# An FFT convolution and MLP kernel: the inverse transforms of two blocks folded once more on VectorE

## The chip, the cores and the metric

The kernel runs on one core of a Trainium2 chip. The core has a matrix engine (TensorE, PE in the profile, with PEld for its weight loads), VectorE (DVE), ScalarE (ACT), GpSimd (POOL) and SyncE (SP), which here only issues transfers. Each engine works through its own queue in order; waits between queues go over semaphores. The metric is the time of one execution on the device in microseconds, lower is better.

## The reference

The input is a sequence of 2048 positions with 512 channels in bf16. Two layers are applied, and in both the same weights and the same `A_k`, `A_v` are used. A layer is a long convolution gated by the normalized input, and then an MLP:

```python
k_shift = sum over t of k_pad[:, t:t + S, :] * shift_k[:, ks - 1 - t]   # 4 taps
kv = k_shift * v
y = irfft(rfft(kv_pad) * rfft(ssm_k_pad))[:S] + kv * ssm_D
x = x + layernorm(x) * y
x = x + (gelu(layernorm(layernorm(x)) @ w1 + b1) @ w2 + b2)    # 512 -> 1376 -> 512
```

The convolution result `y` depends on `k`, `v`, `ssm_k`, `ssm_D` alone, not on `x`, so it is the same in both layers and is computed once.

## The kernel before

**Tiling.** The sequence is cut into 4 blocks of 512 positions. A block lies in SBUF as 128 partitions by 4 positions (position 4p + i on partition p, i = 0 to 3) by 512 channels. The convolution is done by blocks in the frequency domain with a transform of 1024 points of which each block fills half. `forward` (L577 on) turns a block into 256 complex frequencies with matmuls against a table (`R_F`); they lie in two groups of 128 frequencies, numbered c = 0 and 1, each with a real and an imaginary half of 512 channels (ri = 0, 1). Before the change group 0 holds the frequencies 2n + 1/2 and group 1 those at 2n + 3/2. `wrap` joins the spectra of neighbouring filter blocks, `products` multiplies and sums spectra, `inverse` goes back to time with matmuls against a second table (`R_T`) and copies the result to `R_YT`.

**Stages and tags.** In the recorded program each step has a tag: S*b* the shift of block b, K*b* its forward transform, H*m* the spectrum of filter block m, W*m* its wrap, P*b*c0 and P*b*c1 the products of each frequency group, P*b*e the step that combines the products and splits them into two parities o = 0, 1 (time index even or odd), Y*b* the inverse. M*bL*a0 and a1 are the norms and transposes of the MLP of block b in layer L (first and second half of the block), M*bL*b the two matrix products.

**Products.** Block b sums b + 1 products; the first goes straight to the accumulator `R_ACC`, each further one goes to a scratch slot and is added by a DMA that GpSimd issues (L620, `accumulate`). The combining step P*b*e at the end of `products` is four VectorE operations of 2048 elements per partition for blocks 1 to 3 (two groups at once) by the helper `tt` (L557).

**Inverse.** For each half h of the time indices `inverse` issues matmuls of 128x512 over o, c and ri (L575, helper `freq`): 8 per half, 16 per block. The two halves are two PSUM tiles, and ScalarE copies each (L563).

**The MLP.** L779 normalizes on ScalarE, L807 transposes, L824 is the first product (44 matmuls of 512 columns per block, or 88 of 256 where the block is done in halves), L829 the Gelu on ScalarE, L843 the second product (44), L848 (layer 0) and L851 (layer 1) the residual on VectorE. Statistics are L750 and L752 on VectorE; the variance goes to GpSimd for a power of -1/2 (L738; its input is made by L755, L757 or L773) and comes back to VectorE, which makes the shift of the normalization (L739).

**What sets the order.** All operations are recorded first, with what they read and write. `ORDER` is a list of their numbers written out in the file: each engine's queue is the list's operations of that engine in the list's sequence. `BANKS` gives each PSUM tile its bank, and `SIDE` lists the copies that go to VectorE where ScalarE is the default (`copy` with two engines). `replay` runs through the queues with a table of costs to set the waits, and `keep_busy` (its matmul is L913) puts idle matmuls of 128x512 into TensorE's queue where, by those costs, it would stand still for over 700 ns: `k = int(gap * share / cost)`, share 0.8, cost 217.

## Time and profile before

| | |
|---|---|
| median of 3 runs | 245.62 us (245.22 to 245.80) |
| the profiled execution | 244.91 us |
| its span, first to last instruction | 243.1 us |
| TensorE busy, matmuls | 232.9 us, 1551 |
| VectorE busy, instructions | 185.1 us, 357 |
| ScalarE busy, instructions | 181.6 us, 279 |
| mean granted TensorE clock | 0.999 |

A row of the timeline gives the start in us, the time to the end of the last of the merged instructions, the engine, the line, the operation, output and input, the count, and in brackets the idle time just ahead and what ended it. Instructions of one engine overlap a little in the records, so the time from one start to the next is what one costs in a full queue. A row of a stretch (from:to) gives its length, the busy time of PE, PEld, DVE, ACT and POOL with their instruction counts, the granted clock, the share of time in which DMA engines were busy, and GB/s. Busy shares are averages over stages that differ.

### The profile page before, as it was taken

Reading aid. Unit: us, or ns where it says so; the run is one execution under the profiler, and the core shown is the slowest. Engines: PE = TensorE matmul, PEld = TensorE weight load, DVE = VectorE, ACT = ScalarE, POOL = GpSimd, SP = SyncE. Lnnn points to the kernel's source line nnn. Section 1 sums busy time; section 2 is a strip of 40 time slices with the busy share of each in tenths; the row PEclk is TensorE's granted clock in tenths of the full one; section 3 lists DMA queues with packets and bytes.
Section 4 is the critical chain, followed back from the end, with each engine's and each line's share of the span. In section 5 each row is a group of like instructions: output and inputs, shape, how many; then the busy total and the mean of one; then the engine's idle time right before and its main releaser. Section 6 shows DMA issues by size and latency. Waiting matters only on the chain.

```text
span 243.1 us, 3962 instructions
## 1 busy us (share of the span) xinstructions
PE 232.9 (96%) x1551; PEld 131.9 (54%) x1574; DVE 185.1 (76%) x357; ACT 181.6 (75%) x279; POOL 68.0 (28%) x73
## 2 busy tenths in 40 slices
PE   8999996989999999999999999999999999999994
PEld 3756632647655684445444544544468654448841
DVE  1379999999999999999999999783977242574004
ACT  2358998999899589979799285579968657955730
POOL 0000134432572356753146315241310201120000
PEclk9999999999999999999999999999999999999999
DMA  6999916668794099990089989920002000002002
GB/s 189 392 377 220 391 52 238 105 242 162 142 158 62 0 173 173 175 174 3 0 162 185 172 215 226 207 47 3 1 0 89 0 0 3 0 0 86 3 0 86
DMA packets 14406, 29.85 MB, mean 123 GB/s; under 512 B 3026, under 2 KB 8500, under 8 KB 14260
## 3 DMA queue, kind: packets, MB, share of 16 engines
q0 software_dynamic: 5232, 15.21, 32.9%
q1 hardware_dynamic: 9156, 14.40, 17.2%
q8 instruction: 12, 0.20, 0.3%
q14 instruction: 6, 0.05, 0.1%
HBM read 12.30 MB, written 2.10 MB: 59 GB/s over the span
## 4 chain that ended last, share of the span: by engine, by line
PE 67%; DVE 22%; issue 5%; ACT 3%; POOL 2%; DVEq 0%; POOLq 0%
PE ps L824 28%; PE ps L843 26%; DVE ar L557 14%; PE ps L575 6%; DVE sm L750 4%; PE ps L913 3%; PE ps L807 2%; POOL sm L738 2%; ACT ar L779 1%; DVE ar L657 1%; ACT ar L563 1%; DVE ar L851 1%; PE ps L629 1%; PE ps L648 1%; DVE sm L752 1%
## 5 line engine op out<-in xcount | busy, mean ns | idle before, releaser
L557 DVE TENSOR_TENSOR ar<-ar 128x2048 bf16<-128x2048 bf16 (+2 forms) x125 | 115.1, 954 | 9.3 <-ACT ar L563 4.8
L824 PE MATMUL ps<-ar 128*128 128x256 bf16 (+3 forms) x479 | 80.2, 320 | 1.2 <-ACT ar L563 0.9
L563 ACT ACTIVATE ar<-ps 128x1024 bf16<-128x1024 f32 (+2 forms) x61 | 64.3, 1115 | 22.0 <-PE ps L575 10.3
L843 PE MATMUL ps<-ar 128*128 128x512 bf16 (+1 forms) x339 | 79.6, 379 | 0.7
L829 ACT ACTIVATE ar<-ps,sm 128x256 bf16<-128x256 f32 (+3 forms) x121 | 61.5, 572 | 16.5 <-PE ps L824 16.2
L738 POOL TENSOR_TENSOR sm<-sm 128x2 f32<-128x2 f32 x32 | 39.0, 1218 | 104.6 <-DVE sm L757 45.1
L824 PEld LDWEIGHTS ps<-ar 128*128 128x128 bf16 (+1 forms) x484 | 47.7, 100 | 32.3 <-ACT ar L563 1.8
L779 ACT ACTIVATE ar<-ar,sm 128x512 bf16<-128x512 bf16 x64 | 48.4, 808 | 13.3 <-DVE sm L739 13.1
L843 PEld LDWEIGHTS ps<-ar 128*128 128x128 bf16 (+1 forms) x352 | 34.1, 98 | 37.0 <-ACT ar L829 1.2
L575 PE MATMUL ps<-ar 128*128 128x512 bf16 x187 | 44.4, 380 | 3.5 <-ACT ar L563 2.7
L620 POOL DMA_DIRECT2D ar<-ar x30 | 27.5, 931 | 44.8 <-DVE ar L557 25.3
L750 DVE BATCH_NORM_STATS2 sm<-ar 128x6 f32<-128x512 bf16 x48 | 32.5, 687 | 0.4
L575 PEld LDWEIGHTS ps<-ar 128*128 128x128 bf16 x192 | 17.2, 98 | 27.2 <-ACT ar L563 7.7
L851 DVE TENSOR_TENSOR ar<-ps,ar 128x512 bf16<-128x512 f32 x16 | 10.9, 686 | 16.6 <-PE ps L843 16.5
L848 DVE SCALAR_TENSOR_TENSOR ar<-ps,ar 128x512 bf16<-128x512 f32 x16 | 11.0, 685 | 8.4 <-PE ps L843 8.3
L648 PE MATMUL ps<-ar 128*128 128x128 bf16 x256 | 15.6, 219 | 0.3 <-ACT ar L563 0.2
L648 PEld LDWEIGHTS ps<-ar 128*128 128x128 bf16 x256 | 14.7, 98 | 1.8 <-ACT ar L563 0.7
L564 DVE COPY ar<-ps 128x1024 bf16<-128x1024 bf16 (+1 forms) x9 | 7.3, 808 | 7.7 <-PE ps L605 3.9
L771 ACT ACTIVATE ar<-ar,sm 128x512 bf16<-128x512 bf16 x16 | 11.5, 717 | 0.1
L913 PE MATMUL ps<-ar 128*128 128x512 bf16 x34 | 9.4, 428 | 1.0 <-DVE ar L523 1.0
L807 PE MATMUL ps<-ar 128*128 128x128 bf16 x128 | 9.5, 219 | 0.5 <-ACT ar L779 0.4
L807 PEld LDWEIGHTS ps<-ar 128*128 128x128 bf16 x128 | 8.1, 98 | 3.0 <-ACT ar L779 0.9
(27 smaller groups left out, 53.5 us busy)
## 6 DMA issues: line engine op xcount, KB each, us to landing
ar<-ar POOLq DMA_DIRECT2D x24, 512.0 KB, 4.9
ar<-in_A_k_dram SPq DMA_DIRECT2D x4, 512.0 KB, 5.6
ar<-in_A_ssm_k_dram SPq DMA_DIRECT2D x4, 512.0 KB, 8.0
ar<-in_A_v_dram SPq DMA_DIRECT2D x4, 512.0 KB, 5.8
ar<-in_A_q_dram SPq DMA_DIRECT2D x4, 512.0 KB, 7.0
ar<-ar POOLq DMA_DIRECT2D x6, 256.0 KB, 4.6
out_dram<-ar SPq DMA_DIRECT2D x3, 512.0 KB, 2.6
ar<-in_B_w_dram SPq DMA_DIRECT2D x1, 1376.0 KB, 7.1
```

The costliest lines, as they stand in the source:

```text
L557: return P.op(DVE, lambda e: e.tensor_tensor(o, a, b, op), 66.0 + 0.52 * n, reads=[a, b], writes=[o])
L563: return e.activation(dst, src(), AF.Copy)
L575: r = e.matmul(Q(tl, 0, 128, ri * 512, [1, 512]), w, m, start=a, stop=z)
L620: P.op(POOL, lambda e: e.dma_start(dst, src, accum_op=ALU.add), 880.0, reads=[src, dst], writes=[dst], dma=True, nbytes=nb)
L648: r = e.matmul(Q(tl, 0, 128, q, [1, 128]), w, m, start=j == 0, stop=j == 3)
L738: P.op(POOL, lambda e: e.tensor_tensor(r, v, hf, ALU.pow), 1100.0, reads=[v, hf], writes=[r])
L750: P.op(DVE, lambda e, st=st, x=x: e.bn_stats(st, x), 600.0, reads=[x], writes=[st])
L779: P.op(ACT, lambda e: e.activation(o, x, AF.Identity, bias=m, scale=r), 705.0, reads=[x, m, r], writes=[o])
L807: r = e.transpose(QB(tl, 0, 128, 256 * j + 128 * a, [1, 128]), src[4 * a + j], IDN)
L824: r = e.matmul(Q(tl, 0, rows, 0, [1, n]), w, m, start=dk == 0, stop=dk == 3)
L829: P.op(ACT, lambda e, dst=dst, tl=tl, rows=rows, bias=bias, n=n: e.activation(dst, Q(tl, 0, rows, 0, [1, n]), AF.Gelu_apprx_tanh, bias=bia ...
L843: r = e.matmul(Q(tl, 0, 128, 0, [1, 512]), ins[fc][0], ins[fc][1], start=fc == 0, stop=fc == 10)
```

## The change

**The table.** The second frequency group moves from the frequencies 2n + 3/2 to 768 + 2n + 1/2. Modulo 1024 these are the mirror images of the same frequencies, so the group holds the conjugates of the old values in reversed sequence. Since 768 is three quarters of 1024, the two groups' table entries for time index 4p + i differ only by a factor that is a power of the imaginary unit and depends on i alone.

**Wrap.** The sign rule is now the same in both groups: VectorE subtracts in the real half, the accumulating DMA adds in the imaginary half. Before, it was the other way round in group 1.

**Fold.** For blocks 2 and 3 `products` ends with four more VectorE operations of two slices of 512: sums and differences of the two groups, real with real and imaginary with imaginary for o = 0, and crosswise for o = 1. They are written to the free slices of `R_ACC`. `inverse` of these blocks then takes 4 matmuls per half instead of 8. Half 0 reads the sum (z = 0) of o = 0 and both results of o = 1; half 1 reads the difference of o = 0 and both of o = 1. Blocks 0 and 1 are as before.

**Order.** `ORDER`, `BANKS` and `SIDE` are new. `SIDE` has 7 entries for 9: the copies of M20a0 and M31a0 go from VectorE to ScalarE. Lines behind the fold shift by 11: L738 becomes L749, L739 L750, L750 L761, L752 L763, L755 L766, L757 L768, L767 L778, L773 L784, L779 L790, L807 L818, L824 L835, L843 L854, L848 L859, L851 L862, L913 L924.

```diff
 def _tables():
...
-    kk = np.arange(2)[:, None] + 2 * np.arange(128)[None, :]
+    kk = 768 * np.arange(2)[:, None] + 2 * np.arange(128)[None, :]
...
-SIDE = [30, 204, 508, 590, 728, 750, 831, 912, 933]
+SIDE = [30, 204, 512, 736, 758, 839, 941]
...
 ORDER = [
-    0, 1, 2, 3, 28, 4, 5, 6, 7, 8, 9, 10, 11, 44, 12, 13, 27, 45, 14, 15, 16, 17, 18, 46, 19, 20, 21, 22, 29, 97, 48, 202,
+    0, 1, 2, 3, 28, 25, 4, 5, 6, 7, 8, 9, 10, 11, 44, 12, 13, 27, 45, 14, 15, 16, 17, 18, 46, 19, 20, 21, 22, 29, 97, 48, 202,
...
     def wrap(m):
...
-            if c:
-                accumulate(re, pi, 410000)
-                tt(im, im, pr, ALU.subtract, 1024)
-            else:
-                tt(re, re, pi, ALU.subtract, 1024)
-                accumulate(im, pr, 410000)
+            tt(re, re, pi, ALU.subtract, 1024)
+            accumulate(im, pr, 410000)
...
     def products(b):
...
+        if b in (2, 3):
+            for o in range(2):
+                u = A(0, 128, R_ACC + 512 + 1024 * o, [2048, 2], [1, 512])
+                v = A(0, 128, R_ACC + 4608 + 3072 * o, [-2048 if o else 2048, 2], [1, 512])
+                for z in range(2):
+                    tt(A(0, 128, R_ACC + 4096 * z + 1024 * o, [2048, 2], [1, 512]), u, v, ALU.subtract if z else ALU.add, 1024)
 
     def inverse(b):
         tls = [Tile(P, 2) for _ in range(2)]
-        for cs in ((0,), (1,)) if b == 0 else ((0, 1),):
+        if b in (2, 3):
+            for h in range(2):
+                ins = []
+                for o in range(2):
+                    for ri in range(2):
+                        z = h if o == 0 else (h if ri == 0 else 1 - h)
+                        ins.append((o, ri == 0, ri == 1, A(0, 128, R_T + ri * 512 + (2 * h + o) * 128, [1, 128]),
+                                    A(0, 128, R_ACC + 4096 * z + 1024 * o + 2048 * ri, [1, 512])))
+                freq(tls[h], ins)
+        for cs in () if b in (2, 3) else ((0,), (1,)) if b == 0 else ((0, 1),):
```

**How the order moves: the first part.** TensorE, from the forward transforms of block 1 (L575) to the first matmuls of the first MLP (L807, now L818); L913 and L924 are the idle matmuls. Before:

```order
L575 MATMUL ps<-ar 128x512 x36
L913 MATMUL ps<-ar 128x512 x3
L575 MATMUL ps<-ar 128x512 x8
L913 MATMUL ps<-ar 128x512 x7
L575 MATMUL ps<-ar 128x512 x12
L605 MATMUL ps<-ar 128x128 x16
L629 MATMUL ps<-ar 128x128 x16
L575 MATMUL ps<-ar 128x512 x24
L648 MATMUL ps<-ar 128x128 x32
L807 MATMUL ps<-ar 128x128 x8
```

TensorE, the same place now:

```order
L575 MATMUL ps<-ar 128x512 x44
L924 MATMUL ps<-ar 128x512 x10
L575 MATMUL ps<-ar 128x512 x12
L605 MATMUL ps<-ar 128x128 x16
L629 MATMUL ps<-ar 128x128 x16
L575 MATMUL ps<-ar 128x512 x20
L648 MATMUL ps<-ar 128x128 x32
L575 MATMUL ps<-ar 128x512 x4
L924 MATMUL ps<-ar 128x512 x4
L818 MATMUL ps<-ar 128x128 x8
```

Two sets of idle matmuls became one of ten, and a set of four stands ahead of the first MLP transposes; behind these there are none in either order. On VectorE the copy of block 1's transposed `k` (L564, 128x16x128) stood behind one of the first two sums of the first transform and now stands behind both. VectorE, where the first normalization's power is started (L757, now L768) and read back (L739, now L750). Before:

```order
L757 TENSOR_SCALAR sm<-sm 128x2
L557 TENSOR_TENSOR ar<-ar 128x2x1024 x2
L557 TENSOR_TENSOR ar<-ar 128x2x512
L739 SCALAR_TENSOR_TENSOR sm<-sm 128x2 x2
L557 TENSOR_TENSOR ar<-ar 128x2x512
```

VectorE, the same place now:

```order
L768 TENSOR_SCALAR sm<-sm 128x2
L557 TENSOR_TENSOR ar<-ar 128x2x512 x2
L557 TENSOR_TENSOR ar<-ar 128x2048
L557 TENSOR_TENSOR ar<-ar 128x2x1024
L750 SCALAR_TENSOR_TENSOR sm<-sm 128x2 x2
```

One operation of 1024 elements more stands between the start of the power and its two readers.

**Block 2's inverse.** TensorE, from the second product of M10 to that of M01, with the MLP transposes between. Before:

```order
L843 MATMUL ps<-ar 128x512 x10
L807 MATMUL ps<-ar 128x128 x8
L843 MATMUL ps<-ar 128x512 x3
L807 MATMUL ps<-ar 128x128 x8
L575 MATMUL ps<-ar 128x512 x8
L824 MATMUL ps<-ar 128x512 x4
L575 MATMUL ps<-ar 128x512 x8
L824 MATMUL ps<-ar 128x512 x16
```

TensorE, the same place now:

```order
L854 MATMUL ps<-ar 128x512 x15
L818 MATMUL ps<-ar 128x128 x8
L854 MATMUL ps<-ar 128x512 x6
L818 MATMUL ps<-ar 128x128 x8
L575 MATMUL ps<-ar 128x512 x8
L835 MATMUL ps<-ar 128x512 x20
```

Both halves of the inverse, now 4 matmuls each, stand together, and the group of M01 that stood between them follows. VectorE, the combining step of block 2 (the 128x2x2x512 and 128x4x512 operations of L557). Before:

```order
L848 SCALAR_TENSOR_TENSOR ar,sm<-ps,ar 128x512
L739 SCALAR_TENSOR_TENSOR sm<-sm 128x2
L557 TENSOR_TENSOR ar<-ar 128x2x2x512
L739 SCALAR_TENSOR_TENSOR sm<-sm 128x2
L557 TENSOR_TENSOR ar<-ar 128x2x2x512
L739 SCALAR_TENSOR_TENSOR sm<-sm 128x2
L557 TENSOR_TENSOR ar<-ar 128x4x512
L848 SCALAR_TENSOR_TENSOR ar,sm<-ps,ar 128x512
L757 TENSOR_SCALAR sm<-sm 128x2
L557 TENSOR_TENSOR ar<-ar 128x4x512
L848 SCALAR_TENSOR_TENSOR ar,sm<-ps,ar 128x512 x2
```

VectorE, the same place now:

```order
L557 TENSOR_TENSOR ar<-ar 128x2x2x512
L763 BN_AGGR sm<-sm 128x2
L859 SCALAR_TENSOR_TENSOR ar,sm<-ps,ar 128x512
L766 TENSOR_SCALAR sm<-sm 128x2
L750 SCALAR_TENSOR_TENSOR sm<-sm 128x2
L557 TENSOR_TENSOR ar<-ar 128x2x2x512
L750 SCALAR_TENSOR_TENSOR sm<-sm 128x2
L557 TENSOR_TENSOR ar<-ar 128x4x512 x2
L750 SCALAR_TENSOR_TENSOR sm<-sm 128x2
L557 TENSOR_TENSOR ar<-ar 128x2x512 x4
L859 SCALAR_TENSOR_TENSOR ar,sm<-ps,ar 128x512
```

The four folds (128x2x512 x4) follow the combining step directly, and one of the residuals of M10 that stood within it now stands behind the folds.

**Block 3's inverse.** TensorE, from the end of M20's second product to the transposes of M30. Before:

```order
L843 MATMUL ps<-ar 128x512 x10
L824 MATMUL ps<-ar 128x512 x4
L824 MATMUL ps<-ar 96x512 x4
L824 MATMUL ps<-ar 128x512 x32
L575 MATMUL ps<-ar 128x512 x8
L824 MATMUL ps<-ar 128x512 x4
L575 MATMUL ps<-ar 128x512 x8
L843 MATMUL ps<-ar 128x512 x30
L807 MATMUL ps<-ar 128x128 x8
```

TensorE, the same place now:

```order
L854 MATMUL ps<-ar 128x512 x7
L835 MATMUL ps<-ar 96x512 x4
L835 MATMUL ps<-ar 128x512 x40
L575 MATMUL ps<-ar 128x512 x4
L854 MATMUL ps<-ar 128x512 x8
L575 MATMUL ps<-ar 128x512 x4
L854 MATMUL ps<-ar 128x512 x30
L818 MATMUL ps<-ar 128x128 x8
```

The whole first product of M11 now stands ahead of the inverse, and 8 matmuls of its second product stand between the halves. VectorE, the combining step of block 3. Before:

```order
L757 TENSOR_SCALAR sm<-sm 128x2 x2
L557 TENSOR_TENSOR ar<-ar 128x2x2x512 x2
L739 SCALAR_TENSOR_TENSOR sm<-sm 128x2
L557 TENSOR_TENSOR ar<-ar 128x4x512 x2
L773 TENSOR_SCALAR sm<-sm 128x2
L557 TENSOR_TENSOR ar<-ar 128x1024
```

VectorE, the same place now:

```order
L768 TENSOR_SCALAR sm<-sm 128x2
L778 TENSOR_SCALAR sm<-sm 128x2
L557 TENSOR_TENSOR ar<-ar 128x2x2x512 x2
L750 SCALAR_TENSOR_TENSOR sm<-sm 128x2 x2
L557 TENSOR_TENSOR ar<-ar 128x4x512 x2
L784 TENSOR_SCALAR sm<-sm 128x2
L778 TENSOR_SCALAR sm<-sm 128x2
L557 TENSOR_TENSOR ar<-ar 128x2x512 x4
L557 TENSOR_TENSOR ar<-ar 128x1024 x2
```

The folds stand behind the combining step, with three small operations of the statistics between or ahead that stood behind it. In both blocks the fold that writes the difference of o = 0 is the last of the four. SyncE's queue has the same sequence as before, and GpSimd has the same 69 operations in a slightly different one.

2 lines of the change are left out of this document (1 added, 1 removed), and 80 rows, old and new, of the table ORDER.

## The prediction

> **What bounds the kernel now.** I read the page first (busy shares, slices, chain), then the busy times by stage, then the instructions of TensorE and VectorE in order of time around the two places that the change touches.
>
> ```profile
> PE 232.9 (96%) x1551; PEld 131.9 (54%) x1574; DVE 185.1 (76%) x357; ACT 181.6 (75%) x279; POOL 68.0 (28%) x73
> PE   8999996989999999999999999999999999999994
> DVE  1379999999999999999999999783977242574004
> PE 67%; DVE 22%; issue 5%; ACT 3%; POOL 2%; DVEq 0%; POOLq 0%
> ```
>
> By shares alone VectorE (DVE) has a quarter of the span free. The slices say otherwise: it is full from slice 4 to slice 26 and free only behind. The stages show it (columns: PE, PEld, DVE, ACT, POOL busy, then clock):
>
> ```profile
> 67.00:91.00 24.00, 23.23 (x192) 15.33 (x195) 23.93 (x46) 19.93 (x31) 11.00 (x10) 1.00 0.59 99
> 91.00:114.00 23.00, 22.79 (x113) 10.79 (x115) 22.72 (x49) 21.54 (x34) 13.16 (x13) 1.00 0.73 138
> 114.00:140.00 26.00, 25.89 (x138) 12.49 (x138) 25.55 (x46) 19.34 (x32) 10.69 (x12) 1.00 0.64 122
> 140.00:166.00 26.00, 25.84 (x131) 12.48 (x133) 23.18 (x48) 18.34 (x31) 9.15 (x11) 1.00 0.75 163
> 166.00:200.00 34.00, 33.79 (x222) 20.70 (x225) 19.01 (x50) 26.01 (x49) 5.10 (x6) 1.00 0.04 16
> ```
>
> From 67 to 166 us TensorE is busy 97.75 of 99 us and VectorE 95.38 of 99. Behind 166 us only TensorE is full. So a matmul less is worth its time only if VectorE, which gets the folding, does not become the later one. The two inverses are where they meet:
>
> ```profile
> 114.25 1.89 PE L575 MATMUL ps<-ar 128*128 128x512 bf16 x8
> 115.97 1.03 PE L824 MATMUL ps<-ar 128*128 128x512 bf16 x4
> 116.84 1.89 PE L575 MATMUL ps<-ar 128*128 128x512 bf16 x8
> 118.56 8.80 PE L824 MATMUL ps<-ar 128*128 128x512 bf16 x39
> ...
> 166.14 1.89 PE L575 MATMUL ps<-ar 128*128 128x512 bf16 x8
> 167.87 1.03 PE L824 MATMUL ps<-ar 128*128 128x512 bf16 x4
> 168.73 1.89 PE L575 MATMUL ps<-ar 128*128 128x512 bf16 x8
> 170.46 6.64 PE L843 MATMUL ps<-ar 128*128 128x512 bf16 x29
> ```
>
> L575 x8 twice is one inverse: block 2 at 114.25 us, block 3 at 166.14 us. VectorE's side of the same moments, with the rows that the sum below needs:
>
> ```profile
> 112.83 1.22 DVE L557 TENSOR_TENSOR ar<-ar 128x2048 bf16<-128x2048 bf16 x1
> ...
> 163.27 0.16 DVE L739 SCALAR_TENSOR_TENSOR sm<-sm 128x2 f32<-128x2 f32 x1 [0.58 <-POOL sm L738]
> 163.34 2.35 DVE L557 TENSOR_TENSOR ar<-ar 128x2048 bf16<-128x2048 bf16 x2
> 165.62 0.16 DVE L773 TENSOR_SCALAR sm<-sm 128x2 f32<-128x2 f32 x1
> 169.52 0.69 DVE L557 TENSOR_TENSOR ar<-ar 128x1024 bf16<-128x1024 bf16 x1 [3.74 <-ACT ar L563]
> ```
>
> Block 2's last combining step (tag P2e) runs from 112.83 to 114.05, its inverse starts 0.20 later; block 3's (P3e) ends at 163.34 + 2.35 = 165.69, its inverse starts 0.45 later. Both inverses start nearly as soon as VectorE delivers.
>
> **The change, part by part.**
>
> Matmuls. Eight of 128x512 take 115.97 - 114.25 = 1.72 us, 0.215 each. Each of the two inverses issues 8 instead of 16: 16 fewer, -3.44 us of TensorE time, all of it in a stretch where TensorE is full. That is the ceiling.
>
> Fillers. The order has 38 idle matmuls for 34 before: 10 at one place in the early part instead of 3 and 7, and 4 new ones ahead of the first transposes of the MLP. They stand where TensorE would have waited, so their price is between 0 (the wait is there anyway) and 4 x 0.215 = +0.86 us. I take the upper end for the time at which TensorE reaches block 2's inverse, since the same stretch now shows only a short wait at that place (0.41 below).
>
> Folds. Four additions of two slices of 512 each (1024 elements) per block, in front of the inverse. Nearest row:
>
> ```profile
> 78.51 1.29 DVE L557 TENSOR_TENSOR ar<-ar 128x1024 bf16<-128x1024 bf16 x2
> ...
> 14.22 1.20 DVE L657 TENSOR_TENSOR ar<-ps,ar 128x1024 bf16<-128x1024 f32 x1
> ```
>
> The next instruction after the two starts at 79.72, so one costs 0.605 us; four are 2.42, three 1.82. Two of the four read one input with a negative outer step, a form not separately shown; the cost of such a fold is bounded by 0.60 (that row) and 1.20 (a 1024 product that reads PSUM, the slowest of that size). I take 0.60, as the products with swapped halves are in the 2048 group too, whose x2 row above gives 1.14 for twice the elements. The order of the folds leaves the one that the first half of the inverse does not read for last, so the inverse waits for three of the four.
>
> Copies. Two PSUM copies (block 2's first MLP transposes, block 3's of layer 1) go from VectorE to ScalarE. ScalarE pays the duration of its own row, 1.015 each:
>
> ```profile
> L563 ACT ACTIVATE ar<-ps 128x1024 bf16<-128x1024 bf16 x9 | 9.0, 1015 | 6.0 <-PE ps L807 6.0
> 135.19 0.69 DVE L564 COPY ar<-ps 128x1024 bf16<-128x1024 bf16 x1 [0.24 <-PE ps L807]
> 135.80 0.68 DVE L851 TENSOR_TENSOR ar<-ps,ar 128x512 bf16<-128x512 f32 x1
> ```
>
> VectorE is relieved of 0.61 us (135.19 to 135.80) ahead of block 3, and of as much near the end, where it is not full. ScalarE has 26.00 - 19.34 = 6.7 us free from 114 to 140. Behind the two sets of transposes stand ten and seven matmuls of other work (2.15 and 1.5 us), which cover 1.0 as they covered 0.6; if the cover is gone the price is 0.4 each. I put it at 0.
>
> Table and wrap. The second group's wrap keeps one VectorE subtraction and one accumulating DMA per half, only the halves are exchanged: 0. The SP queue's issues stand in the same sequence, GpSimd issues as many DMAs and powers as before. Bounds 0 and, should one accumulation land late, the 0.25 to 0.6 that such waits cost VectorE now.
>
> Order. What matters is what VectorE does ahead of each inverse. Ahead of block 2's: the same work, plus the folds, minus one residual of mlp(1,0) (L848, 0.61, now behind). Ahead of block 3's: all eight folds but the last, minus one copy, plus three small ones of 0.07. TensorE has the same work ahead of block 2's inverse, and ahead of block 3's one group of 4 matmuls of mlp(1,1) more (0.86).
>
> How much of VectorE's own waiting goes away decides the sum. It waits today at these places ahead of 166 us:
>
> ```profile
> 17.60 1.23 DVE L564 COPY ar<-ps 128x2048 bf16<-128x2048 bf16 x1 [0.44 <-PE ps L629]
> 37.53 0.16 DVE L739 SCALAR_TENSOR_TENSOR sm<-sm 128x2 f32<-128x2 f32 x1 [0.52 <-POOL sm L738]
> 54.59 0.62 PE L807 MATMUL ps<-ar 128*128 128x128 bf16 x8 [0.41 <-ACT ar L779]
> 154.65 0.69 DVE L848 SCALAR_TENSOR_TENSOR ar<-ps,ar 128x512 bf16<-128x512 f32 x1 [1.01 <-PE ps L843]
> 157.71 0.69 DVE L848 SCALAR_TENSOR_TENSOR ar<-ps,ar 128x512 bf16<-128x512 f32 x1 [0.28 <-PE ps L843]
> ```
>
> The first goes, since two sums of the first transform now stand ahead of that copy and fill the wait; the second, since the power's reader stands behind two 1024 and two 2048 operations in the new order, 2 x 0.6 + 2 x 1.14 = 3.5 us; 0.24 goes with the copy; 1.01 and 0.28 are waits for TensorE's results by a VectorE that will now arrive later. Together 0.44 + 0.52 + 0.24 + 1.01 + 0.28 = 2.49. The wait of 0.58 for GpSimd I leave.
>
> The sum, against the profiled execution (span 243.1, time 244.91, so 1.8 lie around it; it is 0.71 under the median of the runs, 245.62). Block 2: VectorE is ready at 114.05 + 1.82 - 0.61 - 0.96 = 114.30, plus 0.20; TensorE arrives at 114.25 + 0.86 = 115.11, so TensorE decides. It ends the inverse and the next 4 matmuls 12 x 0.215 = 2.58 later, 117.7 (118.56 before). Then the work up to 166.14, 47.58, and the group moved ahead, 0.86: TensorE is at block 3's inverse at 166.1. VectorE is ready at 165.69 + 2.42 + 1.82 - 0.61 + 0.21 - 2.49 = 167.04, plus 0.2: 167.2. So TensorE waits 1.1 us there and VectorE decides. What follows took 243.1 - 166.14 = 76.96, now less 8 matmuls (1.72) and the group (0.86): 74.38. Span 167.2 + 74.4 = 241.6, which is 1.5 us less. On the median: 244.1 us.
>
> Behind the inverse I expect no new wait: from the end of its first half to the next transposes stand 42 matmuls, 9.0 us, in both orders (4, 8 and 30 before; 8, 4 and 30 now), with VectorE free (3.74 idle at 169.52).
>
> **A rule weighed.** GpSimd's small power, on which every normalization waits, took 1.06 us beside a quiet VectorE, and 3.35 beside back-to-back products; the mean of all is 1.22:
>
> ```profile
> 33.97 2.96 DVE L557 TENSOR_TENSOR ar<-ar 128x2048 bf16<-128x2048 bf16 x3
> 34.15 3.35 POOL L738 TENSOR_TENSOR sm<-sm 128x2 f32<-128x2 f32 x1 [4.95 <-DVE sm L757]
> 174.66 1.06 POOL L738 TENSOR_TENSOR sm<-sm 128x2 f32<-128x2 f32 x1 [0.49 <-DVE sm L773]
> ...
> L738 POOL TENSOR_TENSOR sm<-sm 128x2 f32<-128x2 f32 x32 | 39.0, 1218 | 104.6 <-DVE sm L757 45.1
> ```
>
> The Trainium skill (GPSIMD Engine Reference, section Key points) says that GpSimd shares its SBUF interfaces with VectorE and contends with instructions that have two SBUF inputs; these rows agree. Every fold is such an instruction, so by that rule a power beside four folds is stretched as well, and the sum with a reader right behind would be up to 2.3 us higher (3.35 - 1.06); without such a reader it stays as above. In the new order the readers stand behind 4.2 us of other work after block 3's folds and further behind block 2's, so I add nothing.
>
> **The rivals.**
>
> Full gain: VectorE recovers over 3.4 us and is never waited for. For it: nothing fills the place ahead of the inverses with idle matmuls in the new order. Against it: VectorE's named waits sum to less. TensorE then decides with 3.44 - 0.86 = 2.6 less, 243.0; with the fillers in a wait that exists anyway 242.2.
>
> Gain given back: VectorE recovers only 0.5 to 1.5 us, and TensorE waits for block 3's folds as long as it saves. It gives 243.1 within 0.5 of span, 245.1 to 246.1.
>
> Slower: VectorE recovers none of its waits. Then it is ready at 169.5 + 0.2 = 169.7 for block 3, TensorE waits 3.6 us, span 244.1, time 246.6 on the median. It decides from the point where less than 1.0 us is recovered (169.7 - 168.7, the start at which the span is 243.1 again). For it: VectorE is busy 72.2 of the 73 us from 67 to 140, and a reordered start costs as easily as it gains. Folds at 1.20 for the negative step would add 4 x 0.6 = 2.4 to that.
>
> Power stretched: the two powers whose results VectorE reads ahead of the last products of block 3 hold it 0.58 now; should each take what the slowest took, VectorE and the inverse come about 1.1 later, 245.2. It is this mechanism that the rule above would give; the mean of 1.22 over 32 says that it is rare.
>
> **How the numbers follow.** My forecast, recovery of 1.5 to 3.3 us, has 0.49: 244.1, own range 243.3 to 245.1. Full gain 0.15, given back 0.12, slower 0.20, stretched 0.04. Measurement can tell about 0.2% (0.5 us) from no change. Faster: forecast and full gain, 0.64; the same: given back and stretched, 0.16; slower 0.20. The range reaches from between the two ends of the full gain, 242.6, to the slower case, 246.6.
>
> **What would show it.** In the changed profile: L575 down by 16 matmuls; the two inverses near 115.1 and 167.2 us; a TensorE wait of about 1 us on a VectorE addition ahead of block 3's, none over 0.9 ahead of block 2's; folds at 0.60; the waits at 17.6, 37.5, 154.6 and 157.7 us gone; a span of about 74.4 us from block 3's inverse to the end. The prediction is wrong if the second inverse starts after 168.7, if TensorE waits in the MLPs behind it, or if the first 67 us come out longer by more than the fillers.

## The result, and the profile after

The changed kernel takes 246.11 us (median of 22 runs, 245.44 to 247.06) and the kernel before 245.66 in the same comparison (22 runs, 244.99 to 246.47). The ratio is 1.0016, with an interval of 1.0005 to 1.0028: no gain, and if anything a loss of 0.4 us. The forecast was 244.1. The profiled execution took 246.15 us with a span of 244.3.

From the page of the changed kernel: the busy shares, the shares of the chain that ended last, and two groups.

```profile
PE 234.2 (96%) x1562; PEld 129.7 (53%) x1562; DVE 187.2 (77%) x363; ACT 182.8 (75%) x281; POOL 72.3 (30%) x73
...
PE 43%; DVE 33%; POOL 10%; DMA 7%; issue 3%; ACT 2%; POOLq 0%
...
L575 PE MATMUL ps<-ar 128*128 128x512 bf16 x176 | 42.3, 380 | 2.8 <-ACT ar L563 2.0
...
L749 POOL TENSOR_TENSOR sm<-sm 128x2 f32<-128x2 f32 x32 | 40.6, 1270 | 80.1 <-DVE sm L766 45.5
```

L575 is down from 192 to 176 matmuls: the fold does what it says. The chain is what changed. TensorE held 67% of it and GpSimd 2%; now TensorE holds 43%, VectorE 33%, GpSimd 10% and DMA 7%. The same chain in order of time, a stretch ahead of block 2, shows a new path through GpSimd (columns: start, time on the chain, engine, output, line).

```profile
97.83 2.78 POOL sm L749
100.61 4.56 DMA ar<-ar
105.51 5.90 DMA ar<-ar
111.43 1.23 DVE ar L557
```

A power (L749) holds up the accumulating DMA that GpSimd issues behind it, and block 2's combining step waits for the next one.

**Where executions differ from the start.** The start up to VectorE's first copy shifts from one execution to the next: a profile with an early copy is one that ran under its own kernel's median by about as much (before: copy at 11.62, time 244.91 against 245.66; q_stats_later below: copy at 13.01, 246.42 against 245.53). VectorE's first copy, before and after:

```profile
11.62 1.23 DVE L564 COPY ar<-ps 128x2048 bf16<-128x2048 bf16 x1 [3.93 <-PE ps L605]
```

```profile
12.29 1.23 DVE L564 COPY ar<-ps 128x2048 bf16<-128x2048 bf16 x1 [4.06 <-PE ps L605]
```

So landmarks below are counted from that copy. Before, block 2's inverse stood at 114.25 - 11.62 = 102.63 and block 3's at 166.14 - 11.62 = 154.52. After (TensorE's timeline):

```profile
55.62 0.62 PE L818 MATMUL ps<-ar 128*128 128x128 bf16 x8 [0.56 <-ACT ar L790]
...
71.95 0.62 PE L818 MATMUL ps<-ar 128*128 128x128 bf16 x8 [0.57 <-ACT ar L790]
...
117.19 2.10 PE L575 MATMUL ps<-ar 128*128 128x512 bf16 x8
119.12 9.66 PE L835 MATMUL ps<-ar 128*128 128x512 bf16 x44
...
157.06 0.62 PE L818 MATMUL ps<-ar 128*128 128x128 bf16 x8 [0.79 <-ACT ar L790]
...
169.94 1.03 PE L575 MATMUL ps<-ar 128*128 128x512 bf16 x4
```

Block 2's inverse is at 117.19 - 12.29 = 104.90, 2.27 later than before, and block 3's at 169.94 - 12.29 = 157.65, 3.13 later. From block 3's inverse to the end it takes 244.3 - 169.94 = 74.36 for 76.96 before, 2.60 less. The sum, +0.53 from the first copy on, is near the +0.45 of the medians.

VectorE's timeline shows what is late: the bracket is the wait ahead of a row.

```profile
36.18 0.16 DVE L750 SCALAR_TENSOR_TENSOR sm<-sm 128x2 f32<-128x2 f32 x1 [0.52 <-POOL sm L749]
...
63.94 0.16 DVE L750 SCALAR_TENSOR_TENSOR sm<-sm 128x2 f32<-128x2 f32 x1 [0.28 <-POOL sm L749]
...
70.18 0.16 DVE L750 SCALAR_TENSOR_TENSOR sm<-sm 128x2 f32<-128x2 f32 x1 [0.51 <-POOL sm L749]
...
100.68 0.16 DVE L750 SCALAR_TENSOR_TENSOR sm<-sm 128x2 f32<-128x2 f32 x1 [0.52 <-POOL sm L749]
...
111.43 1.23 DVE L557 TENSOR_TENSOR ar<-ar 128x2048 bf16<-128x2048 bf16 x1 [0.36 <-DMA ar<-ar]
...
115.09 2.49 DVE L557 TENSOR_TENSOR ar<-ar 128x1024 bf16<-128x1024 bf16 x4
...
134.70 0.16 DVE L750 SCALAR_TENSOR_TENSOR sm<-sm 128x2 f32<-128x2 f32 x1 [0.58 <-POOL sm L749]
...
152.82 0.69 DVE L761 BATCH_NORM_STATS2 sm<-ar 128x6 f32<-128x512 bf16 x1 [0.82 <-DMA ar<-in_A_q_dram]
...
155.29 0.16 DVE L750 SCALAR_TENSOR_TENSOR sm<-sm 128x2 f32<-128x2 f32 x1 [0.58 <-POOL sm L749]
...
167.28 2.48 DVE L557 TENSOR_TENSOR ar<-ar 128x1024 bf16<-128x1024 bf16 x4
```

The waits for TensorE that the forecast saw (1.01 and 0.28 near 155 us) are gone. There are now six waits for a GpSimd power, one for an accumulating DMA (0.36; 0.25 before) and one for the load of a later block's input. The six are 2.99 us; before there were three, of 0.52, 0.58 and one of 0.31 that the forecast had passed over, 1.41. By the busy times of the two stretches from the first copy (columns as in the prediction's stages), VectorE's idle time rose a little in sum. Before:

```profile
11.62:112.83 101.21, 95.86 (x733) 56.08 (x740) 98.85 (x179) 88.70 (x118) 38.88 (x36) 1.00 0.72 173
112.83:165.69 52.86, 52.54 (x276) 25.62 (x280) 49.81 (x95) 38.54 (x63) 20.70 (x21) 1.00 0.69 140
```

After:

```profile
12.29:115.09 102.80, 97.81 (x743) 55.49 (x741) 99.32 (x178) 86.91 (x115) 43.58 (x36) 1.00 0.70 170
115.09:169.10 54.01, 53.05 (x280) 24.95 (x278) 51.85 (x104) 42.08 (x69) 21.15 (x21) 1.00 0.68 137
```

Ahead of block 2 it stands still 102.80 - 99.32 = 3.48 for 101.21 - 98.85 = 2.36, and between there and block 3's folds 2.16 for 3.05: together 5.64 for 5.41.

GpSimd's timeline at those places shows why its results come late:

```profile
32.27 3.88 POOL L749 TENSOR_TENSOR sm<-sm 128x2 f32<-128x2 f32 x1 [3.87 <-DVE sm L768]
...
59.89 3.22 POOL L549 CAST sm<-ar 96x1 f32<-96x1 bf16 x1
63.19 0.72 POOL L749 TENSOR_TENSOR sm<-sm 128x2 f32<-128x2 f32 x1
...
67.41 2.74 POOL L749 TENSOR_TENSOR sm<-sm 128x2 f32<-128x2 f32 x1
...
97.83 2.82 POOL L749 TENSOR_TENSOR sm<-sm 128x2 f32<-128x2 f32 x1 [0.20 <-DVE sm L784]
...
205.68 0.69 POOL L749 TENSOR_TENSOR sm<-sm 128x2 f32<-128x2 f32 x1 [11.62 <-DVE sm L784]
```

The same power takes 0.69 us where VectorE does nothing (205.68) and 2.7 to 3.9 beside VectorE's products.

### The profile page after: what moved, and what is told of

It is laid out like the page before. It is cut to its first block, busy times and chain, and to the rows that moved or that the text cites. A ratio compares the mean times of both kernels' runs of the same rounds, so it can differ in the third digit from the quotient of the medians.

```text
span 244.3 us, 3974 instructions
## 1 busy us (share of the span) xinstructions
PE 234.2 (96%) x1562; PEld 129.7 (53%) x1562; DVE 187.2 (77%) x363; ACT 182.8 (75%) x281; POOL 72.3 (30%) x73
## 4 chain that ended last, share of the span: by engine, by line
PE 43%; DVE 33%; POOL 10%; DMA 7%; issue 3%; ACT 2%; POOLq 0%
DVE ar L557 24%; PE ps L854 18%; PE ps L835 17%; DMA ar<-ar 7%; POOL sm L749 6%; DVE sm L761 3%; PE ps L924 3%; POOL ar L620 3%; PE ps L575 3%; DVE ar L862 2%; PE ps L818 1%; ACT ar L790 1%; POOL sm L549 1%; DVE ar L859 1%; DVE ar L564 1%
## 5 line engine op out<-in xcount | busy, mean ns | idle before, releaser
L557 DVE TENSOR_TENSOR ar<-ar 128x2048 bf16<-128x2048 bf16 (+2 forms) x133 | 119.7, 934 | 9.4 <-ACT ar L790 5.5
L854 PE MATMUL ps<-ar 128*128 128x512 bf16 (+1 forms) x352 | 81.5, 379 | 0.2
L563 ACT ACTIVATE ar<-ps 128x1024 bf16<-128x1024 f32 (+2 forms) x63 | 65.8, 1117 | 20.6 <-PE ps L575 10.9
L835 PE MATMUL ps<-ar 128*128 128x256 bf16 (+3 forms) x484 | 80.6, 321 | 0.6 <-ACT ar L563 0.6
L840 ACT ACTIVATE ar<-ps,sm 128x256 bf16<-128x256 f32 (+3 forms) x121 | 61.6, 569 | 13.3 <-PE ps L835 12.9
L835 PEld LDWEIGHTS ps<-ar 128*128 128x128 bf16 (+1 forms) x484 | 47.6, 100 | 32.6 <-ACT ar L563 2.1
L749 POOL TENSOR_TENSOR sm<-sm 128x2 f32<-128x2 f32 x32 | 40.6, 1270 | 80.1 <-DVE sm L766 45.5
L790 ACT ACTIVATE ar<-ar,sm 128x512 bf16<-128x512 bf16 x64 | 49.0, 813 | 14.2 <-DVE sm L750 14.2
L854 PEld LDWEIGHTS ps<-ar 128*128 128x128 bf16 (+1 forms) x352 | 33.9, 98 | 37.7 <-ACT ar L840 1.1
L575 PE MATMUL ps<-ar 128*128 128x512 bf16 x176 | 42.3, 380 | 2.8 <-ACT ar L563 2.0
L620 POOL DMA_DIRECT2D ar<-ar x30 | 28.1, 1035 | 42.3 <-DVE ar L557 28.8
L761 DVE BATCH_NORM_STATS2 sm<-ar 128x6 f32<-128x512 bf16 x48 | 31.9, 683 | 1.1 <-DMA ar<-in_A_q_dram 0.8
L575 PEld LDWEIGHTS ps<-ar 128*128 128x128 bf16 x176 | 15.2, 98 | 25.7 <-ACT ar L563 7.8
L862 DVE TENSOR_TENSOR ar<-ps,ar 128x512 bf16<-128x512 f32 x16 | 10.7, 685 | 16.5 <-PE ps L854 16.4
L859 DVE SCALAR_TENSOR_TENSOR ar<-ps,ar 128x512 bf16<-128x512 f32 x16 | 10.9, 680 | 8.7 <-PE ps L854 8.5
L648 PEld LDWEIGHTS ps<-ar 128*128 128x128 bf16 x256 | 14.6, 98 | 1.2 <-issue 0.6
L782 ACT ACTIVATE ar<-ar,sm 128x512 bf16<-128x512 bf16 x16 | 11.6, 723 | 3.6 <-DVE sm L778 3.1
L818 PE MATMUL ps<-ar 128*128 128x128 bf16 x128 | 9.7, 220 | 2.3 <-ACT ar L790 2.2
L924 PE MATMUL ps<-ar 128*128 128x512 bf16 x38 | 10.9, 444 | 1.0 <-DVE ar L523 1.0
L818 PEld LDWEIGHTS ps<-ar 128*128 128x128 bf16 x128 | 7.9, 98 | 6.3 <-ACT ar L790 4.8
L549 POOL CAST sm<-ar 128x10 f32<-128x10 bf16 (+1 forms) x2 | 3.7, 1848 | 23.3 <-DMA ar<-in_B_b_dram 23.3
```

The costliest lines, as they stand in the source:

```text
L557: return P.op(DVE, lambda e: e.tensor_tensor(o, a, b, op), 66.0 + 0.52 * n, reads=[a, b], writes=[o])
L563: return e.activation(dst, src(), AF.Copy)
L575: r = e.matmul(Q(tl, 0, 128, ri * 512, [1, 512]), w, m, start=a, stop=z)
L620: P.op(POOL, lambda e: e.dma_start(dst, src, accum_op=ALU.add), 880.0, reads=[src, dst], writes=[dst], dma=True, nbytes=nb)
L648: r = e.matmul(Q(tl, 0, 128, q, [1, 128]), w, m, start=j == 0, stop=j == 3)
L749: P.op(POOL, lambda e: e.tensor_tensor(r, v, hf, ALU.pow), 1100.0, reads=[v, hf], writes=[r])
```

## The experiments

The account to be tested: the fold itself is worth about what the sum said, and the new order spends it on readers of a power (and of a load) that stand directly behind the products which hold the power up. The rivals: the fold costs VectorE too much whatever the order; the four idle matmuls cost 0.86; the accumulating DMAs are the limit. All kernels, with the ratio to the kernel before on the same chip, and, counted in us from VectorE's first copy in the profiled execution, the starts of the two inverses and the end:

| kernel | median us | ratio [interval] | block 2 | block 3 | end |
|---|---|---|---|---|---|
| before | 245.66 | 1 | 102.63 | 154.52 | 231.48 |
| changed | 246.11 | 1.0016 [1.0005, 1.0028] | 104.90 | 157.65 | 232.01 |
| fold_old_order | 247.25 | 1.0072 [1.0054, 1.0090] | 104.52 | 157.62 | 232.99 |
| new_order_no_fold | 249.07 | 1.0139 [1.0116, 1.0163] | 104.90 | 158.49 | 234.65 |
| cast_early | 245.88 | 1.0016 [1.0001, 1.0031] | 104.64 | 157.36 | 231.74 |
| q_stats_later | 245.53 | 1.0005 [0.9989, 1.0020] | 104.92 | 157.20 | 231.59 |
| thin_fold_old_order | 245.20 | 0.9981 [0.9959, 1.0002] | 102.95 | 155.38 | 231.07 |
| thin_fold_new_order | 245.65 | 1.0009 [0.9993, 1.0025] | 104.93 | 157.18 | 231.61 |
| no_power | 243.19 | 0.9905 [0.9884, 0.9926] | 103.20 | 154.80 | 229.20 |
| cast_and_stats | 245.34 | 0.9989 [0.9972, 1.0005] | 104.66 | 156.59 | 230.95 |
| no_power_before | 245.35 | 0.9986 [0.9970, 1.0003] | 102.31 | 154.20 | 231.20 |
| moves_no_four | 245.37 | 0.9968 [0.9952, 0.9985] | 104.65 | 156.57 | 230.93 |
| moves_swaps | 243.52 | 0.9911 [0.9889, 0.9933] | 103.73 | 155.40 | 229.78 |
| swaps_before | 245.40 | 0.9979 [0.9967, 0.9992] | 102.40 | 154.29 | 231.28 |

**The fold in the order before.** `ORDER`, `SIDE` and `BANKS` are those of the kernel before, with the folds directly behind the combining steps.

```diff
-SIDE = [30, 204, 512, 736, 758, 839, 941]
+SIDE = [30, 204, 512, 594, 736, 758, 839, 920, 941]
...
 ORDER = [
-    0, 1, 2, 3, 28, 25, 4, 5, 6, 7, 8, 9, 10, 11, 44, 12, 13, 27, 45, 14, 15, 16, 17, 18, 46, 19, 20, 21, 22, 29, 97, 48, 202,
+    0, 1, 2, 3, 28, 4, 5, 6, 7, 8, 9, 10, 11, 44, 12, 13, 27, 45, 14, 15, 16, 17, 18, 46, 19, 20, 21, 22, 29, 97, 48, 202, 30,
...
```

> The fold alone: the order, banks and copies of the kernel before, with the new table and wrap, and the four folds put directly behind the combining step of blocks 2 and 3. Theory 1 (VectorE has no room there, so the fold pays only if the order around it changes): block 2's inverse starts 1.8 us later than before, near 116.1, block 3's between 168.6 and 170.1, and with about 74.4 us behind it the time is 246.4 to 247.9. Theory 2 (the fold is worth what was forecast, and the new order is what lost it): block 3's inverse near 167.2, time about 244.1, clearly under the kernel before.

It came out at 247.25 us. TensorE's timeline:

```profile
117.03 1.04 PE L575 MATMUL ps<-ar 128*128 128x512 bf16 x4 [0.43 <-DVE ar L557]
...
170.13 1.04 PE L575 MATMUL ps<-ar 128*128 128x512 bf16 x4
```

Block 2's inverse now starts with a wait for the folds and 1.89 us later than before, about three folds (1.82), and block 3's 3.10 later, as theory 1 said. In the old order VectorE makes up nothing ahead of block 2, so a new order was needed; it is not the new order alone that costs. One thing blurs the price: the cost table put 16 idle matmuls into this queue behind 70 us that the kernel before has not. Six stand ahead of each inverse, where TensorE would have waited for the folds, but the four at 126.54 (0.86 us) may cost time; the thin folds below leave all of them out.

**The new order without the fold.** The kernel before, with the changed kernel's order less the eight folds.

```diff
-SIDE = [30, 204, 508, 590, 728, 750, 831, 912, 933]
+SIDE = [30, 204, 508, 728, 750, 831, 933]
...
 ORDER = [
-    0, 1, 2, 3, 28, 4, 5, 6, 7, 8, 9, 10, 11, 44, 12, 13, 27, 45, 14, 15, 16, 17, 18, 46, 19, 20, 21, 22, 29, 97, 48, 202,
+    0, 1, 2, 3, 28, 25, 4, 5, 6, 7, 8, 9, 10, 11, 44, 12, 13, 27, 45, 14, 15, 16, 17, 18, 46, 19, 20, 21, 22, 29, 97, 48,
...
```

> The new order alone: order, banks and copies of the changed kernel, with the old table and wrap, no folds, and 16 matmuls per inverse again. Theory 1 (the first part of the new order is late of itself, by norms that come late from GpSimd): block 2's inverse starts near 117, as in the changed kernel, although no fold stands ahead of it; 32 matmuls against 16 make the two inverses 3.4 us longer, less what VectorE no longer delays by 8 x 0.6, so the time is 248 to 249.5. Theory 2 (the folds themselves delay block 2's inverse): it starts near 115, and the time is under 247.5.

249.07 us, as theory 1 said, and 3.4 more than before with the same inverse of 16 matmuls per block: that is what the new order costs by itself. Against the changed kernel it is 1.0139 - 1.0016 = 1.2%, 3.0 us: within the new order the fold is worth most of its 3.44. TensorE's inverse of block 2, both halves:

```profile
117.55 3.62 PE L575 MATMUL ps<-ar 128*128 128x512 bf16 x16
```

Its first copy is at 12.65, so this is 104.90, as in the changed kernel, though VectorE had no fold to do here. So ahead of block 2 it is not the folds that make TensorE late, but something in the order before it.

**The cast moved.** The 96x1 cast (3.22 us at 59.89) stands ahead of a power; here it is issued far earlier (operation 24; the line that it leaves is not shown).

```diff
-    101, 83, 66, 23, 86, 125, 102, 71, 89, 212, 69, 103, 87, 65, 214, 213, 218, 90, 215, 216, 126, 104, 70, 219, 245, 438,
+    101, 83, 66, 23, 24, 86, 125, 102, 71, 89, 212, 69, 103, 87, 65, 214, 213, 218, 90, 215, 216, 126, 104, 70, 219, 245, 438,
...
```

> The changed kernel with one GpSimd operation moved: the cast of the last 96 biases, which took 3.2 us at 59.9 us beside nine VectorE products, now stands right behind the other cast at 25 us. Theory 1 (GpSimd's queue is what delays the norms of the first MLP): the power at 67.4 us comes 2.5 to 3 us earlier, TensorE's wait of 0.57 at 72 us and VectorE's of 0.51 at 70 us go, and the time falls by 0.5 or more, to 245.6 or less. Theory 3 (VectorE's full queue sets the pace there, and GpSimd only fills what is left): the power moves, the time does not, 246.1.

The ratio is the changed kernel's, 1.0016, as theory 3 said. VectorE's wait of 0.28 goes and TensorE's of 0.57 falls to 0.31, but VectorE's 0.51 stays. GpSimd's timeline:

```profile
60.48 3.73 POOL L749 TENSOR_TENSOR sm<-sm 128x2 f32<-128x2 f32 x1
```

The power moved up into the place of the cast and now takes 3.73 itself. So it is not the cast as such that is long: the power, too, is long when it starts there beside VectorE's products.

**The statistics of the late input moved.** Operation 715, a statistic of the input whose load came 0.82 late, stands behind 698.

```diff
-    639, 503, 630, 696, 626, 643, 504, 697, 648, 527, 505, 715, 528, 640, 506, 698, 644, 507, 529, 737, 531, 641, 508, 699,
+    639, 503, 630, 696, 626, 643, 504, 697, 648, 527, 505, 528, 640, 506, 698, 715, 644, 507, 529, 737, 531, 641, 508, 699,
```

> The changed kernel with one VectorE operation moved: the first statistics of block 3 for the MLP, for which VectorE stood 0.82 us at 152 us waiting for the load of q, now stand two operations later. Theory 1 (this wait is what delays the norms of M11 and makes TensorE wait 0.79 at 157): both waits go, and the time falls by 0.5 to 0.8, to 245.3 to 245.6. Theory 3 (GpSimd's power and the accumulating DMA ahead of it are late anyway): TensorE waits as long as before, time 246.1.

VectorE's timeline at the place of the 0.82 wait:

```profile
153.45 1.23 DVE L557 TENSOR_TENSOR ar<-ar 128x2048 bf16<-128x2048 bf16 x1 [0.48 <-DMA ar<-ar]
```

The wait for the load is gone, and the next in line, an accumulating DMA, takes 0.48 of it. TensorE's wait of 0.79 falls to 0.31, and block 3's inverse is 0.45 earlier. The ratio of 1.0005 can't be told from the changed kernel's by its interval, so the runs don't decide between the two theories.

**Thin folds, both orders.** The folds work on 2 elements of each slice instead of 512, so the inverse gets the right number of operations and VectorE nearly no work. With the order before, idle matmuls are kept out behind 70 us.

```diff
-                u = A(0, 128, R_ACC + 512 + 1024 * o, [2048, 2], [1, 512])
+                u = A(0, 128, R_ACC + 512 + 1024 * o, [2048, 2], [1, 2])
...
-            k = int(gap * share / cost) if gap > least else 0
+            k = int(gap * share / cost) if gap > least and t < 70000 else 0
```

> The fold in the order of the kernel before, as in fold_old_order, but each fold works on 2 elements per slice instead of 512 (the rest of the sums is left out), so VectorE pays some 0.1 us instead of 0.6 for each, and no idle matmuls stand behind the first 70 us. Theory 1 (VectorE's time for the folds is all that stands against the saved matmuls): block 2's inverse starts as long after the first transform's copy as before, and both inverses are 1.72 shorter: 3.4 us less than before, 242.1. Rival (the accumulating DMA and GpSimd's powers are next in line, so the saving cannot be had there even with folds that cost nothing): 243.5 to 245.

> The changed kernel with folds of 2 elements per slice instead of 512 (the rest of the sums is left out). Theory 1 (the new order's first part is late of itself): block 2's inverse starts where it did, 104.9 us after VectorE's first copy, and the time falls by 0.5 to 1.0 only, through the waits behind it: 245.1 to 245.6. Rival (the folds hold TensorE up through VectorE): the time falls by 2 us or more, to 244 or less.

Folds that cost VectorE nearly nothing should have given the full gain of 3.44 us in the old order. They gave 0.5 (0.9981, an interval that reaches 1): 245.20 is just above even the rival's 243.5 to 245. VectorE's timeline there:

```profile
154.77 1.23 DVE L557 TENSOR_TENSOR ar<-ar 128x2048 bf16<-128x2048 bf16 x1 [1.10 <-DMA ar<-ar]
...
162.53 2.36 DVE L557 TENSOR_TENSOR ar<-ar 128x2048 bf16<-128x2048 bf16 x2 [1.02 <-DMA ar<-ar]
```

So in the old order the accumulating DMAs stand next behind VectorE (1.10 and 1.02 in one stretch), and block 3's inverse comes 155.38 - 154.52 = 0.86 later than before although TensorE has 8 matmuls less ahead of it. (The record of that inverse counts 3 of its 4 matmuls, so 0.2 of the 0.86 may be the record.) In the new order thin folds leave block 2's inverse at 104.93, and the time at 245.65, as theory 1 said: once more, not the folds.

**The powers taken away.** VectorE multiplies by a half where GpSimd raised to a power; in the changed kernel and in the kernel before.

```diff
-        P.op(POOL, lambda e: e.tensor_tensor(r, v, hf, ALU.pow), 1100.0, reads=[v, hf], writes=[r])
+        P.op(DVE, lambda e: e.tensor_scalar(r, v, 0.5, None, ALU.mult), 90.0, reads=[v], writes=[r])
```

> The changed kernel with GpSimd's 32 powers left out and a VectorE multiplication of the same two numbers in their place (the normalization is thus left out in part). Theory 1 (GpSimd's power, stretched beside VectorE's products, delays VectorE and the norms in the first 117 us): VectorE's six waits for it (3.0 us) go against 32 x 0.07 = 2.2 us of new work, block 2's inverse starts 1 us or more earlier, time 245.2 or less. Rival (VectorE's own full queue sets the pace and hides these waits): 246 to 247.5, by the work added.

> The kernel before with GpSimd's 32 powers left out and a VectorE multiplication of the same two numbers in their place (the normalization is thus left out in part), the counterpart of no_power (243.2). Theory 1 (the saved matmuls of the fold are given back to GpSimd's powers, and without these they count): 244.7 to 245.6 here, since VectorE's waits for a power are 1.4 us here and the multiplications cost 2.2; the pair without powers then differs by 1.5 us or more in favour of the fold, against 0.45 the other way with them. Rival (the powers cost both kernels the same, and the fold's saving goes elsewhere): 242.7 to 243.2 here, no difference between the two.

With 32 small operations more on VectorE the changed kernel falls to 243.19 us (0.9905); the kernel before hardly moves (245.35, 0.9986). Theory 1 said so in both cases. TensorE's and then VectorE's timeline of the changed kernel without powers:

```profile
115.30 1.89 PE L575 MATMUL ps<-ar 128*128 128x512 bf16 x8
...
166.90 1.03 PE L575 MATMUL ps<-ar 128*128 128x512 bf16 x4
```

```profile
150.31 0.69 DVE L761 BATCH_NORM_STATS2 sm<-ar 128x6 f32<-128x512 bf16 x1 [0.77 <-DMA ar<-in_A_q_dram]
```

The first copy is at 12.10: both inverses come earlier, by 1.7 and 2.85 us. The row at 150.31 is the only wait of over 0.2 us that VectorE has left between 20 and 165 us. Without powers fold and new order together are worth 0.9986 - 0.9905 = 0.8%, 2.0 us, and the two intervals don't overlap. This takes away more than the readers' waits, since GpSimd's queue is also free for its DMA issues; the next ones part the two.

**Both moves, then the idle matmuls.** The two moves of above together; and with them the limit for idle matmuls raised, so that the set of four ahead of the first MLP transposes isn't put in.

```diff
-    P.keep_busy(lambda e: e.matmul(idle, zero, zeros, start=True, stop=True), 217.0, 700.0, 0.8, cleared)
+    P.keep_busy(lambda e: e.matmul(idle, zero, zeros, start=True, stop=True), 217.0, 1400.0, 0.8, cleared)
```

> Both single moves together, the cast of cast_early and the statistics of q_stats_later. If the two effects add (0.2 and 0.6 against the changed kernel), 245.3, which would be level with the kernel before or 0.2 under it; if the second wait hides the first, 245.5.

> The changed kernel with the two moves of cast_and_stats and without the four new idle matmuls ahead of the first MLP transposes. If these stand in a wait that is there anyway (0.56 behind them in the changed kernel), the time is that of cast_and_stats, 245.3; if they cost their 0.86, it is 244.5.

The moves together bring 245.34 us (0.9989). Without the four, TensorE's timeline at their place:

```profile
55.91 0.62 PE L818 MATMUL ps<-ar 128*128 128x128 bf16 x8 [1.42 <-ACT ar L790]
```

The wait of 0.56 became 1.42, by just the 0.86 of four matmuls, and the end is where it was (230.93 for 230.95 from the first copy). The ratios of the two, measured against the kernel before on different chips, overlap by their intervals. By the landmarks the four cost nothing: the forecast's upper end was the wrong one.

**The readers moved by one operation.** On top of that, three readers of a power (L750) change places with the VectorE operation behind them (parts of the lines of `ORDER`).

```diff
-    215, 216, 126, 104, 70, 219,
+    215, 216, 126, 70, 104, 219,
...
-    381, 137, 269, 166,
+    381, 269, 137, 166,
...
-    574, 301, 284, 420,
+    574, 284, 301, 420,
```

> As moves_no_four, and in three places where VectorE stood 0.51 to 0.52 us waiting for a power (36, 70 and 101 us) the reader now stands behind the next operation of 0.6 us. Theory 1 (VectorE's waits for powers are what was lost ahead of block 2's inverse): VectorE gains up to 1.5 us, block 2's inverse starts 1.0 to 1.5 earlier than 104.9 after the first copy, and the time falls to 244.3 or less. Rival (the norms come later by as much, and TensorE waits for these, not for the folds): 245.3, as without the swaps.

243.52 us, 0.9911, as theory 1 said: better than both kernels, and three exchanges take it there from 0.9968. VectorE's timeline at the first of them, and behind it GpSimd's:

```profile
31.77 3.55 DVE L557 TENSOR_TENSOR ar<-ar 128x1024 bf16<-128x1024 bf16 x4
35.24 0.15 DVE L750 SCALAR_TENSOR_TENSOR sm<-sm 128x2 f32<-128x2 f32 x1
35.32 0.68 DVE L557 TENSOR_TENSOR ar<-ar 128x1024 bf16<-128x1024 bf16 x1
35.92 0.16 DVE L750 SCALAR_TENSOR_TENSOR sm<-sm 128x2 f32<-128x2 f32 x1
```

```profile
32.00 3.88 POOL L749 TENSOR_TENSOR sm<-sm 128x2 f32<-128x2 f32 x1 [3.87 <-DVE sm L768]
```

The power is as long as in the changed kernel (3.88), but its end at 35.88 now falls under a product, and its reader at 35.92 doesn't wait. The waits of 0.52, 0.51 and 0.52 are gone, and with them the 0.36 for the DMA; in its place VectorE waits 0.47 for TensorE at 108.79. What is next in line ahead of block 3 is another DMA, with TensorE's inverses below it:

```profile
161.78 1.23 DVE L557 TENSOR_TENSOR ar<-ar 128x2048 bf16<-128x2048 bf16 x1 [0.66 <-DMA ar<-ar]
```

```profile
115.75 1.89 PE L575 MATMUL ps<-ar 128*128 128x512 bf16 x8
...
167.42 1.04 PE L575 MATMUL ps<-ar 128*128 128x512 bf16 x4
```

From a first copy at 12.02 these are 103.73 and 155.40, 0.9 and 1.2 earlier than without the exchanges.

**The same exchanges in the kernel before.** Three readers there change places in the same way (parts of the lines of `ORDER`).

```diff
-    92, 126, 104, 70, 105,
+    92, 126, 70, 104, 105,
...
-    503, 525, 729, 526,
+    503, 729, 525, 526,
...
-    531, 713, 700, 549,
+    531, 700, 713, 549,
```

> The counterpart of moves_swaps on the kernel before: in its three places where VectorE waits for a power (0.52 at 37.5, 0.31 at 150.9 and 0.58 at 163.3 us) the reader stands behind the next operation. Theory 1 (without the fold TensorE is the later one, so VectorE's waits are worth little): 245.0 to 245.6, and the fold with swaps (243.5) stays 1.5 us or more ahead. Rival (any order gains as much from such swaps, and the fold is worth nothing): 244.4 or less.

0.9979, half a microsecond, as theory 1 said. So the better version isn't good for the exchanges alone: with the readers out of the way in both, fold and new order together with the two moves are worth 0.9979 - 0.9911 = 0.7%, 1.7 us. The pair isn't quite even, since the kernel before got no such moves, and in the new order these are worth 0.3 to 0.5% (0.9989 and 0.9968 against 1.0016). The pair without powers has no moves on either side, and there it is 2.0.

## Why the prediction was wrong

**Right.** The 16 matmuls; the folds at 0.60 (four in 2.49 at block 2, and the next operation starts 117.50 - 115.09 = 2.41 behind the first; the negative step too); the copy ahead of block 3 at nothing (TensorE shows no wait behind the transposes at 135.97); the waits of 0.44, 0.24, 1.01 and 0.28 gone; the stretch behind block 3's inverse, 74.38 forecast and 74.36 measured.

**Partly right.** Idle matmuls: the forecast put 0.86 into TensorE's arrival at block 2; it is 0 by the landmarks of the experiment that took them out.

**The step that failed** is "how much of VectorE's own waiting goes away". The forecast let 2.49 us of it go. In the two stretches above it rose from 5.41 to 5.64, a miss of 2.72. The wait of 0.52 for the first power, which the forecast let go since "the power's reader stands behind two 1024 and two 2048 operations", stayed at 0.52: the power lengthened with the work in front of its reader, from 3.35 to 3.88. The 0.58 at 163.27, which the forecast left in, did go. And waits came that the old order didn't have: 0.28, 0.51 and 0.52 for powers and 0.36 (0.25 before) for a DMA ahead of block 2; 0.58 twice and 0.82 behind. VectorE's work, in turn, rose by 151.17 - 148.66 = 2.51 where the sum had 3.84; why it is 1.33 less, though as many folds stand there as were counted, stays open. By line, 0.94 of it lies in the statistics of the norms (L750 and L752 before): as many operations, whose busy time fell from 24.17 to 23.71 and from 5.94 to 5.46. Both together make the third fold of block 3 ready at 169.10 - 12.29 = 156.81 from the first copy, where the forecast had 167.04 - 11.62 = 155.42: 1.39 late.

**A second step failed: TensorE was late too.** It was to wait 1.1 us for block 3's folds. It came itself at 157.65, 0.84 behind them, with no wait, so TensorE's own lateness set the time; with TensorE there in time the inverse would have started some 0.6 earlier, by the forecast's 0.2 from fold to inverse. It was 104.90 - 103.49 = 1.41 late already at block 2 (115.11 - 11.62 = 103.49), and this not for the folds: without folds and with thin ones it arrives there at the same time, without powers 1.7 earlier and with three readers moved 0.9 earlier. Since the idle matmuls in that 103.49 cost nothing, what has to be explained is the whole 2.27 against the kernel before. Norms that VectorE finishes late reach TensorE as waits for ScalarE (0.56 and 0.57 ahead of block 2, 0.79 at 157.06), for which the forecast had no term. The timelines of ScalarE and of TensorE's weight loads show one more such path ahead of block 2:

```profile
100.88 0.81 ACT L790 ACTIVATE ar<-ar,sm 128x512 bf16<-128x512 bf16 x1 [0.59 <-DVE sm L750]
...
102.89 0.55 PEld L575 LDWEIGHTS ps<-ar 128*128 128x128 bf16 x4 [0.67 <-ACT ar L840]
```

ScalarE's normalization waits for the reader of 100.68, the Gelu (L840) comes behind it, and TensorE's weight loads wait for the Gelu 0.67 here and 0.61 and 0.42 at 104.05 and 105.88; the kernel before waits 0.19 at that place. From M10's first product to block 2's inverse TensorE takes 117.19 - 92.92 = 24.27 for 114.25 - 91.11 = 23.14 with the same matmuls (the first row before counts 43 of its 44, so 0.2 of the difference may be the record). With the readers moved the same waits are still there (0.69, 0.61 and 0.42), and this stretch still takes 115.75 - 91.69 = 24.06 (43 of 44 again), 0.92 longer than before, of the 1.10 by which that inverse is still late.

**The rival that came true in kind** is the stretched power, to which 0.04 was given and which was looked for ahead of block 3's last products. It struck at other places, ahead of block 2 and in the norms between. The rule weighed there was applied to the folds alone, and beside these no reader waited. For the first power the forecast trusted that its reader stands behind enough other work. That was the wrong test: other work behind which the reader stands, when it is products, is what holds the power up. Two readings helped the error along. The power "beside a quiet VectorE", 1.06 at 174.66, ran beside a product of 174.48; alone it takes 0.69 in the kernel before too (at 204.89). And a mean of 1.22 is no sign that long ones are rare: at least nine of the 32 took 1.45 to 3.35 there. Of the other cases, "given back" (245.1 to 246.1) has the time about right, but by its condition, how much VectorE recovers, "slower" (nothing recovered, 246.6) is the nearer; neither has TensorE itself late.

**What is shown and what is argued.** That waits on powers take the gain is shown by two kinds of experiment (powers gone, readers moved) in both kernels. How an execution without folds in the new order can be as late at block 2 as one with them is shown as a fact, and that its readers' waits are the reason only by what moving them gave, 0.9 of the 2.27 us, or 1.2 with the two moves. The rest has its place, the stretch with the waits for the Gelu, but no run changed the sequence there, so its cause stays open. Taking the powers away also frees GpSimd's queue, and the exchanges alone do not say what that is worth.

## What to carry to other kernels

When work is moved to an engine that is full, look in the new order at what stands directly ahead of every operation that reads another engine's result: there a few hundred nanoseconds each time give back what the matmuls saved. A short helper operation on GpSimd is priced by what VectorE does meanwhile, not by its mean, and one more operation between the products and the reader was enough cover at the six places tried here. Changing places in the order by one can be worth as much as a change in arithmetic: three exchanges gave 0.6% in the new order, and 0.2% in the old one, where TensorE was the later engine.
